# Moving a dozen output stores and three small transposes between queues in a block-sparse attention and gated MLP kernel

## The chip, the cores and the metric

The kernel runs on one core of one Trainium2 chip. The metric is the device time of one execution in microseconds (us); lower is better. The engines are TensorE (PE; its weight loads are listed as PEld), VectorE (DVE), ScalarE (ACT), GpSimd (POOL) and SyncE (SP). SP computes nothing: it issues DMAs.

## What is computed

Two stages in a row. The first is attention over 4 batches, 8 heads, 768 positions and 64 dimensions per head. Positions are grouped in 24 blocks of 32. A block of queries sees its neighbouring blocks, the first and the last block, and three sampled blocks; the first and the last query block see everything. The attention output, with its heads side by side, is the input x (4 x 768 x 512) of the second stage, a gated MLP:

```python
h = np.maximum(x @ w_in, 0.0)                       # 512 -> 1024
u, v = h[..., :512], h[..., 512:]
v_n = (v - mean(v)) / sqrt(var(v) + 1e-6)
v_s = einsum('ts,bsd->btd', w_spatial, v_n) + b_spatial[None, :, None]
out = (u * v_s) @ w_out                             # 512 -> 512, float32
```

## The kernel before

**Tiles.** Two heads make a pair; there are 16 pairs, four to a batch. The 768 positions are six chunks of 128. Keys and queries are loaded in float32, cast to bf16 and transposed, so that `kq` holds head dimension by position; 24 more rows of `kq` carry the block mask. The scores are computed transposed (keys on partitions), the exponential runs on ScalarE from PSUM into `a_all`, and a second product with `vv` (values with a column of ones beside them) gives the output and its row sum. DVE divides and writes `xn`, which has queries on partitions. For the MLP, x is needed transposed, as `xt` (features on partitions, 768 positions), one `xt` tile for each pair.

**Order.** The program is written out as slots, and each engine executes its own instructions in the order in which they are written. A slot holds one group of score matmuls, one group of value matmuls, and whatever tables attach to it: `at[s]` (before the MLP's steps of that slot), the MLP steps themselves (`run_queue(STEPS.get(s))`, one step is one matmul), and `late[s]` (behind them). Slots 0 to 35 are batch 0, slots 36 to 179 batches 1 to 3 with twelve slots to a pair, `S0` is 36.

**Batch 0** is cut in thirds of the query positions, 256 each. A *unit* is one pair and one third: units 0 and 1 are the two heads of pair 0 with its first two thirds; units 2 to 7 are pairs 1 to 3 with the first and the second third; units 8 to 11 are pairs 0 to 3 with the last third. `av_unit` ends with the division into `xn_ref[u]` (tag `xn3`, three buffers). `xtr_third(u)` then turns that x into its columns of `xt`: `xtr_pe` transposes chunk by chunk on TensorE into an unused part of the same PSUM tile, and DVE copies the result. The table `XT_AT` says behind which slot; a unit without an entry has slot `3 * u + 7`, which is 31, 34 and 37 for units 8, 9 and 10. The pairs of batches 1 to 3 take a different way: `xtr_dma` transposes all six chunks with one DMA on SP's queue.

**The MLP of batch 0** runs inside the slots of batches 0 and 1. The products `v4` and `v5` (chunks 4 and 5, the last third) are dealt at slot 42. One product is four matmuls, one for each pair, into one PSUM bank: slot 42 has the first of `v4` (pair 0), slot 43 the other three (pairs 1, 2, 3). Then come `u4` and `u5`, the spatial product (`s_product`), whose gated result is transposed by DMA on SP, and the output product (`o_product`). Each output product ends in a copy to an `osb` tile (six buffers) and a store of 256 KB to `out`. With `ST_ACT` empty for batches 0 and 1, their stores are on SP's queue. The six stores of batch 0 are written at slots 84, 88, 91, 93, 95 and 97, those of batch 1 at 136, 138, 140, 142, 143 and 145.

**SP's queue** carries nearly all DMAs. From slot 20 to 44 it has, in this order: the transpose of pair 4's k and q (`tr_dma`, L448, slot 20), the loads of pair 5 (slot 22), two transposes of the spatial weight (`ws_tr`, L593, slots 23 and 27), `tr_dma` of pair 5 (slot 31), the loads of pair 6 (slot 31), the third `ws_tr` (slot 31), the loads of pair 7 (slot 38), `tr_dma` of pair 6 (slot 40) and the loads of the output weight (slot 44).

**GpSimd's queue** has casts: k, q and v of each later pair (`cast`, L138), the spatial weight (`ws_cast`, L589), weights of the MLP, and the small reciprocal root of the normalisation (L661, L663). For pair p from 7 on, with g = 36 + 12 (p - 4), the casts are at slot g - 24 and the kq transpose at g - 20 (g - 16 for pairs 10 and 14). No DMA is issued from GpSimd.

The functions that the change touches, with what calls them:

Of the kernel before, what the change touches and what calls it, by code (L numbers as in the profile page):

```python
# [26 lines left out]
def kernel(  # L27
# [16 lines left out]
    nc = tc.nc  # L44
# [19 lines left out]
    TC = NCH // NT  # L64
    TW = TC * 128
# [154 lines left out]
    def dve_copy(o, i):  # L220
        nc.vector.tensor_copy(out=o, in_=i)  # L221
# [82 lines left out]
    def bank(nm="ps", tag=None):  # L304
        return psum.tile([128, 1024], BF16, tag=tag or moe_tag(), bufs=2 if tag else 1, name=nm)

    def tr(ps, c, in_):
        nc.tensor.transpose(out=ps[:, c * 128:(c + 1) * 128], in_=in_, identity=ident)  # L308

    def pair_of(src, c):  # L310
        return src[:, c].rearrange("p h d -> p (h d)")
# [143 lines left out]
    a_ref, av_ref, x_ref, xn_ref, xt_ref = {}, {}, {}, {}, {}  # L455
# [96 lines left out]
    def xt_tile(p):  # L552
        if p not in xt_ref:
            xt_ref[p] = work.tile([128, S], BF16, tag="xt", bufs=7, name="xt")
        return xt_ref[p]

    def xtr_pe(p, xn, c0, n, ps=None):
        if ps is None:
            ps = bank()
        for c in range(n):  # L560
            tr(ps, c, pair_of(xn, c))
        dve_copy(xt_tile(p)[:, c0 * 128:(c0 + n) * 128], ps[:, 0:n * 128])

    def xtr_third(u):
        t, p = UNITS[u]
        if t == "h":
            if p == 1:
                xtr_pe(0, xn_ref.pop(0), 0, 2 * TC)
        else:
            xtr_pe(p, xn_ref.pop(u), t * TC, TC, x_ref.pop(u))  # L570

# [42 lines left out]
    def product(n, lhs, rhs, last, done, w=512):  # L614
        ref = {}
        out = []
        for i in range(n):
            def run(i=i):
                if i == 0:
                    ref["ps"] = moe_ps(last)  # L620
                nc.tensor.matmul(out=ref["ps"][:, 0:w], lhsT=lhs(i), rhs=rhs(i),  # L621
                                 start=(i == 0), stop=(i == n - 1))
                if i == n - 1:
                    done(ref["ps"][:, 0:w])
            out.append(run)
        return out
# [3 lines left out]
    ST_ACT = [(), (), (4,), (0, 1, 2)]  # L630
# [3 lines left out]
    class Moe:  # L634
# [75 lines left out]
        def o_product(self, tcc):  # L710
            steps = []
            osb = {}
            parts = 2 if self.last and tcc == NCH - 1 else 1
            w = DM // parts
            for i in range(parts):
                cs = slice(i * w, (i + 1) * w)

                def done(ps, i=i, cs=cs):
                    if i == 0:
                        osb["t"] = work.tile([128, DM], FP32, tag="osb", bufs=6, name="osb")  # L720
                    on_act = (tcc + i) % 2 == 0 if self.last else tcc in O_ACT[self.b]
                    (act_copy if on_act else dve_copy)(osb["t"][:, cs], ps)
                    (nc.scalar if i or tcc in ST_ACT[self.b] else nc.sync).dma_start(
                        out=out[self.b].rearrange("(p c) d -> c p d", c=NCH)[tcc][:, cs],
                        in_=osb["t"][:, cs])
                steps += product(NDH, lambda d: self.gt[:, tcc, d, :],
                                 lambda d, cs=cs: w_out_t[:, d, cs], self.last, done, w)
            return steps
# [42 lines left out]
    def when(slot, *fns):  # L771
        at.setdefault(slot, []).extend(fns)

    def c(f, *a, **kw):
        return lambda: f(*a, **kw)
# [14 lines left out]
    when(2, staged)  # L790
    for p, sl in ((3, 18), (0, 21)):
        when(sl, c(tr_rest, p, 2 if p == 0 else 1))
    XT_AT = {1: 12, 3: 15, 5: 23, 11: 41}
    for u in range(1, len(UNITS)):
        late.setdefault(XT_AT.get(u, 3 * u + 7), []).append(c(xtr_third, u))
    late[12].append(c(tr_rest, 1))
# [134 lines left out]
```

## Time and profile before

| | |
|---|---|
| Median of 3 runs | 208.25 us (208.04 to 208.35) |
| The profiled execution's own time | 208.44 us |
| Its span in the profile | 206.7 us, 5245 instructions |
| Busy in the span | PE 97%, ACT 81%, DVE 64%, POOL 36% |
| DMA | 42.41 MB, nearly all on SP's queue |

The profile is one execution, recorded by the hardware. A row of a timeline has the start in us from the start of the span, the duration, the engine, the line of the program, the operation, the tile written and the tile read, and at the end, in brackets, how long the engine was idle before and what released it. Rows that follow each other with the same form are merged (x2). "SPq" is SP's queue of DMA issues: its duration is how long SP was held by the issue, not how long the data took. The view of one tile also gives the time from issue to landing as minimum, median and maximum. In the table of groups the figures behind the bar are total busy time, mean duration in ns, and idle time of the engine just before instructions of the group. Matmuls overlap, so the end of one lies beyond the start of the next.

### The profile page before, as it was taken

The page shows a single profiled execution, that of the slowest core. Times are in us where ns is not written, and L with a number is a line of the kernel's source. Part 1 is how long each engine was busy: PE and PEld are TensorE (multiplying, and loading weights), DVE is VectorE, ACT ScalarE, POOL GpSimd, SP SyncE. Part 2 cuts the span into 40 slices and gives each one's busy share as a digit, 9 for nine tenths or more (in the row PEclk, how much of TensorE's full clock was granted, in tenths as well). Part 3 has the DMA queues.
Part 4 walks back from the last instruction along what each step waited for, and adds up shares of the span by engine and source line. Part 5 has one row for each costly group of instructions (what it writes and reads, how often), then busy time and mean ns, then how long its engine had stood idle before and what let it go on. Part 6 is the DMA issues. An engine that isn't in the chain of part 4 may idle for free.

```text
span 206.7 us, 5245 instructions
## 1 busy us (share of the span) xinstructions
PE 201.2 (97%) x2122; PEld 126.4 (61%) x2122; DVE 131.4 (64%) x287; ACT 166.8 (81%) x222; POOL 74.4 (36%) x116
## 2 busy tenths in 40 slices
PE   8899999999999999999999999999999999999993
PEld 6679878766666666655655556655565656444441
DVE  7588797989654363648797355448686444576542
ACT  6999999999999999889999887998989883166021
POOL 6799799574680413210716401300202000013000
PEclk9999999999999999999999999999999999999999
DMA  5999999999999989999986749985101062960266
GB/s 140 355 362 359 326 410 270 235 250 333 267 357 201 251 242 203 325 308 271 285 113 172 174 89 264 205 236 127 38 3 38 0 92 51 162 235 0 44 163 251
DMA packets 66363, 42.41 MB, mean 205 GB/s; under 512 B 47524, under 2 KB 61220, under 8 KB 66340
## 3 DMA queue, kind: packets, MB, share of 16 engines
q1 hardware_dynamic: 65332, 40.71, 78.2%
q10 hardware_dynamic: 1008, 1.38, 1.8%
q8 instruction: 16, 0.26, 0.5%
q14 instruction: 7, 0.06, 0.1%
HBM read 24.38 MB, written 6.29 MB: 148 GB/s over the span
## 4 chain that ended last, share of the span: by engine, by line
PE 92%; DMA 3%; DVE 2%; SPq 1%; issue 0%; ACT 0%; ACTq 0%
PE ps_moe L621 33%; PE ps L491 23%; PE ps_av L542 13%; PE ps_t L621 8%; PE ps L478 6%; PE ps_sc L621 5%; PE ps_av L524 4%; DMA st_v<-in_v_dram 3%; DVE kq L221 1%; SPq L110 1%; PE ps L308 1%; PE ps_av L308 1%; DVE vv L138 1%; SPq L143 0%; DVE xn L507 0%
## 5 line engine op out<-in xcount | busy, mean ns | idle before, releaser
L495 ACT ACTIVATE a_all<-ps 128x768 bf16<-128x768 f32 x144 | 112.6, 812 | 11.7 <-PE ps L491 5.2
L491 PE MATMUL ps<-kq 88*128 88x384 bf16 x288 | 70.4, 325 | 0.0
L542 PEld LDWEIGHTS <-a_all 128*128 128x128 bf16 x864 | 45.2, 97 | 20.0
L542 PE MATMUL ps_av<-vv,a_all 128*128 128x65 bf16 x864 | 49.8, 193 | 0.0
L491 PEld LDWEIGHTS <-kq 88*128 88x128 bf16 x288 | 27.9, 97 | 29.0
L621 PE MATMUL ps_moe<-w_in_t,xt 128*128 128x512 bf16 x144 | 43.2, 378 | 0.0
L483 ACT ACTIVATE a_all<-ps 128x1024 bf16<-128x1024 f32 x36 | 34.0, 1026 | 1.5 <-PE ps L478 1.3
L621 PE MATMUL ps_moe<-vn,w_spt 128*128 128x512 bf16 x108 | 33.5, 378 | 0.0
L661 POOL TENSOR_SCALAR std<-mv 128x3 f32<-128x3 f32 (+1 forms) x9 | 2.9, 317 | 69.4 <-DVE mv L658 54.8
L138 POOL CAST nat<-st_k 128x768 bf16<-128x768 f32 (+2 forms) x18 | 13.8, 769 | 31.5 <-DMA st_k<-in_k_dram 30.4
L694 DVE SCALAR_TENSOR_TENSOR un<-ps_moe,b_col,un 128x512 bf16<-128x512 f32 x18 | 13.5, 749 | 14.8 <-PE ps_moe L621 14.8
L478 PE MATMUL ps<-kq 88*128 88x256 bf16 (+3 forms) x140 | 21.6, 275 | 1.2 <-DVE kq L221 0.5
L506 DVE RECIPROCAL rc<-ps_av 128x6 f32<-128x6 f32 (+1 forms) x36 | 6.7, 185 | 24.7 <-PE ps_av L542 23.2
L621 PEld LDWEIGHTS <-xt 128*128 128x128 bf16 x192 | 15.5, 98 | 7.8 <-issue 0.2
L507 DVE TENSOR_TENSOR xn<-ps_av,rc 128x384 bf16<-128x384 f32 (+1 forms) x36 | 18.5, 513 | 1.2
L621 PE MATMUL ps_moe<-w_out_t,gt 128*128 128x512 bf16 x60 | 18.1, 378 | 0.0
L657 DVE BATCH_NORM_STATS2 stats<-vn 128x6 f32<-128x512 bf16 x24 | 16.4, 684 | 1.3 <-ACT vn L652 0.9
L138 POOL CAST nat<-st_q 128x768 bf16<-128x768 f32 (+2 forms) x21 | 14.9, 708 | 3.8 <-DMA st_q<-in_q_dram 3.3
L478 PEld LDWEIGHTS <-kq 88*128 88x128 bf16 (+1 forms) x140 | 12.6, 97 | 5.6 <-DVE kq L221 1.6
L221 DVE COPY kq<-tt 64x1536 bf16<-64x1536 bf16 x24 | 15.1, 630 | 0.4
L188 DVE TENSOR_SCALAR vn<-ps_moe 128x512 bf16<-128x512 f32 x18 | 12.4, 686 | 4.7 <-PE ps_moe L621 4.6
L621 PEld LDWEIGHTS <-w_spt 128*128 128x128 bf16 x144 | 11.7, 98 | 5.2
(86 smaller groups left out, 208.1 us busy)
## 6 DMA issues: line engine op xcount, KB each, us to landing
st_v<-in_v_dram SPq DMA_DIRECT2D x16, 384.0 KB, 5.9
st_k<-in_k_dram SPq DMA_DIRECT2D x15, 384.0 KB, 5.0
out_dram<-osb SPq DMA_DIRECT2D x19, 256.0 KB, 2.7
st_q<-in_q_dram SPq DMA_DIRECT2D x12, 384.0 KB, 4.7
w_f<-in_moe_w_in_dram SPq DMA_DIRECT2D x6, 256.0 KB, 6.7
ws_f<-in_moe_w_spatial_dram SPq DMA_DIRECT2D x4, 384.0 KB, 7.5
out_dram<-osb ACTq DMA_DIRECT2D x4, 256.0 KB, 2.3
st_q<-in_q_dram SPq DMA_DIRECT2D x6, 128.0 KB, 5.6
```

The lines of the kernel that those rows point to most:

```text
L138: eng.tensor_copy(out=dst, in_=src)
L188: nc.vector.tensor_scalar(out=out, in0=in0, scalar1=s1, scalar2=s2, op0=o0, **kw)
L221: nc.vector.tensor_copy(out=o, in_=i)
L478: nc.tensor.matmul(out=ps[:, at:at + n * TW], lhsT=kq[0:kr, h, ci * 128:(ci + 1) * 128], rhs=kq[0:kr, h, qcols(t0, n)], start=True, stop=True)
L483: nc.scalar.activation(out=out, in_=ps, func=AF.Exp, scale=0.125)
L491: nc.tensor.matmul(out=ps[:, hf * 512:hf * 512 + HALF], lhsT=kq[0:KR, j % H, ci * 128:(ci + 1) * 128], rhs=kq[0:KR, j % H, S + hf * HALF:S ...
L495: nc.scalar.activation(out=a_ref["h", j][:, ci, :].rearrange("p (b c) -> p b c", b=2), in_=ps.rearrange("p (b c) -> p b c", b=2)[:, :, 0:H ...
L507: nc.vector.tensor_tensor(out=out, in0=ps[:, :, 0:D], in1=rc[:, 0:n].to_broadcast([128, n, D]), op=ALU.mult)
L542: nc.tensor.matmul(out=av_ref[j][:, qc, 0:VA], lhsT=a_ref["h", j][:, ci, qc * 128:(qc + 1) * 128], rhs=vv[p % NVV][:, h, ci, 0:VA], start= ...
L621: nc.tensor.matmul(out=ref["ps"][:, 0:w], lhsT=lhs(i), rhs=rhs(i), start=(i == 0), stop=(i == n - 1))
L657: nc.vector.bn_stats(out=stats, in_=self.vn[:, tcc, :])
L694: nc.vector.scalar_tensor_tensor(out=self.un[:, tcc, :], in0=ps, scalar=b_col[:, tcc:tcc + 1], in1=self.un[:, tcc, :], op0=ALU.add, op1=AL ...
```

## The change

Two edits. The stores of batches 0 and 1 (twelve, 256 KB each) are issued from GpSimd's queue; those of batches 2 and 3 stay where they were. And for units 8, 9 and 10 (pairs 0 to 2, last third) the x transpose on TensorE with its copy on DVE is replaced by one DMA transpose of two chunks each, on SP's queue; with it, these three move from behind slots 31, 34 and 37 to behind slots 29, 32 and 35, each the slot in which its `xn` is written. Unit 11 stays on TensorE, at slot 41.

```diff
@@ xtr_third
         if t == "h":
             if p == 1:
                 xtr_pe(0, xn_ref.pop(0), 0, 2 * TC)
+        elif t == 2 and p < 3:
+            nc.sync.dma_start_transpose(
+                out=xt_tile(p)[:, t * TW:(t + 1) * TW].rearrange("p (c n) -> p c n", c=TC),
+                in_=xn_ref.pop(u).rearrange("p c h d -> p (c h d)"))
         else:
             xtr_pe(p, xn_ref.pop(u), t * TC, TC, x_ref.pop(u))
@@ o_product
-                    (nc.scalar if i or tcc in ST_ACT[self.b] else nc.sync).dma_start(
+                    (nc.gpsimd if self.b < 2 else
+                     nc.scalar if i or tcc in ST_ACT[self.b] else nc.sync).dma_start(
                         out=out[self.b].rearrange("(p c) d -> c p d", c=NCH)[tcc][:, cs],
                         in_=osb["t"][:, cs])
@@ tables
-    XT_AT = {1: 12, 3: 15, 5: 23, 11: 41}
+    XT_AT = {1: 12, 3: 15, 5: 23, 8: 29, 9: 32, 10: 35, 11: 41}
```

## The prediction

> **What bounds the kernel now.** I read the page first, then the timelines of TensorE and of SP's DMA queue around the third query thirds of batch 0, then the tiles that the change touches. The page:
>
> ```profile
> PE 201.2 (97%) x2122; PEld 126.4 (61%) x2122; DVE 131.4 (64%) x287; ACT 166.8 (81%) x222; POOL 74.4 (36%) x116
> PE 92%; DMA 3%; DVE 2%; SPq 1%; issue 0%; ACT 0%; ACTq 0%
> L491 PE MATMUL ps<-kq 88*128 88x384 bf16 x288 | 70.4, 325 | 0.0
> ```
>
> TensorE is 92% of the chain that ended last, and the largest group of its matmuls (the scores of batches 1 to 3) has 0.0 us of idle time ahead of it: nothing that TensorE needs comes late. Two things follow. Work taken from SP, DVE or GpSimd buys nothing unless TensorE has less to do. And a wait put into TensorE's stream costs its whole length, since no later idle time can give it back.
>
> SP's DMA queue executes in program order, and in the stretch that the change touches it is full:
>
> ```profile
> 33.57 5.47 SPq L593 DMA_TRANSPOSE w_spt<-ws_b  x2
> 39.13 2.89 SPq L448 DMA_TRANSPOSE tt<-nat  x1
> 42.07 0.58 SPq L110 DMA_DIRECT2D st_k<-in_k_dram  x1
> ...
> 43.20 0.47 SPq L110 DMA_DIRECT2D st_v<-in_v_dram  x1
> 44.13 2.84 SPq L593 DMA_TRANSPOSE w_spt<-ws_b  x1
> 47.01 0.58 SPq L110 DMA_DIRECT2D st_k<-in_k_dram  x1
> ...
> 48.74 3.45 SPq L448 DMA_TRANSPOSE tt<-nat  x1
> ```
>
> The order is that of the slots in the code: the first two transposes of the spatial weight (slots 23 and 27), the kq transpose of pair 5 (slot 31), the three loads of pair 6 (slot 31), the third weight transpose (slot 31), the loads of pair 7 (slot 38), the kq transpose of pair 6 (slot 40).
>
> **Part one: three x transposes go from TensorE to SP's queue.** Units 8, 9 and 10 are pairs 0, 1 and 2 of the last query third. Their x is read by the products v4 and v5, which are dealt at slot 42: one matmul in slot 42 (pair 0), three in slot 43 (pairs 1, 2 and 3). In TensorE's timeline these are the first two L621 rows here:
>
> ```profile
> 45.38 0.38 PE L621 MATMUL ps_moe<-w_in_t,xt 128*128 128x512 bf16 x1
> 45.60 0.49 PE L491 MATMUL ps<-kq 88*128 88x384 bf16 x2
> 45.93 0.35 PE L542 MATMUL ps_av<-vv,a_all 128*128 128x65 bf16 x6
> 46.11 0.81 PE L621 MATMUL ps_moe<-w_in_t,xt 128*128 128x512 bf16 x3
> 46.76 0.49 PE L491 MATMUL ps<-kq 88*128 88x384 bf16 x2
> ```
>
> Three matmuls take 46.76 - 46.11 = 0.65, or 0.22 each: pair 0 is needed at 45.38, pair 1 at 46.11, pair 2 at 46.33.
>
> Removed: two transposes on TensorE and one copy on DVE for each of the three units. One of each:
>
> ```profile
> 36.33 0.27 PE L308 MATMUL ps_av<-ident,xn 128*128 128x128 bf16 x2
> 38.18 0.27 DVE L221 COPY xt<-ps_av 128x256 bf16<-128x256 bf16 x1
> ```
>
> At most 3 x 0.27 = 0.8 us of TensorE (the 0.27 holds the drain of the pipeline too, which overlaps what follows) and 0.8 us of DVE. I credit neither separately: below, the end is set by when a transfer lands, not by how early TensorE gets there.
>
> Added: three DMA transposes of two 128x128 blocks on SP, after slots 29, 32 and 35. Their place among the other entries is what matters. Unit 8 comes before the kq transpose of pair 5. Units 9 and 10 come behind it, behind pair 6's loads and **behind the third weight transpose**, ahead of pair 7's loads. Their inputs are ready early, so they don't wait for data; what holds the weight transpose ahead of them is a cast on GpSimd:
>
> ```profile
> 34.74 0.42 DVE L507 TENSOR_TENSOR xn<-ps_av,rc 128x256 bf16<-128x256 f32 x1
> ...
> 40.57 0.43 DVE L507 TENSOR_TENSOR xn<-ps_av,rc 128x256 bf16<-128x256 f32 x1
> 41.02 3.08 POOL L589 CAST ws_b<-ws_f 128x768 bf16<-128x768 f32 x2 [2.00 <-DMA w_spt<-ws_b]
> ```
>
> Unit 8's xn is there at 35.16, unit 10's (the last of the three) at 41.00, the cast at 44.10. No row shows a two-block transpose. The nearest are the six-block x transposes of the later batches, and one eight-block transpose of the gated product in the tail with nothing else in flight:
>
> ```profile
> L573 SPq DMA_TRANSPOSE xt<-xn x12: 1210/1246/1831, 59.6 to 176.9; - x12
> DMA to landing us min/median/max: 2.7/3.7/5.8
> gt<-un SPq DMA_TRANSPOSE x1, 3.1
> w_spt<-ws_b SPq DMA_TRANSPOSE x1, 5.7
> ```
>
> SP is held 1.21 to 1.83 for six blocks. A third of the blocks may take a third of that, 0.40; I take 1.2, as the shortest and the median of the row are the same, which looks like a fixed price. From issue to landing I take 3.1, between the row's 2.7 and its median 3.7, because blocks are few but a weight transpose is just ahead. The sum along SP's queue, with gaps of 0.05 as in the rows:
>
> - The second weight transpose ends at 39.04. Unit 8: 39.1 to 40.3, landing 42.2, ahead of its need at 45.38. No stall there.
> - Kq transpose of pair 5: 40.35 + 2.89 = 43.24. Loads of pair 6 (43.67 - 42.07 = 1.60): 43.3 to 44.9.
> - Third weight transpose (cast long done): 44.95 + 2.84 = 47.8.
> - Unit 9: 47.85 to 49.05, landing 50.95, needed at 46.11.
> - Unit 10: **49.1** to 50.3, landing **52.2**, needed at 46.33.
>
> TensorE is in order. Behind the waiting product stand the scores of slot 44 and all else; ScalarE can finish what is in its two PSUM buffers and then has nothing. So the second matmul of slot 43 moves from 46.33 to 52.2, **5.9 us**, and by the page all behind it moves as well.
>
> Bounds: with SP held 0.40 each, unit 8 ends at 39.5, the kq transpose at 42.4, the loads at 44.1, the weight transpose at 47.0, and unit 10 is issued at 47.45; at 2.7 it lands at 50.15, a stall of 3.8. The weight transpose ahead (5.7 from 44.13) lands at 49.8, so little less is possible on shared queues. With 1.83 each, unit 10 is issued near 50.4; at 5.8 it lands at 56.2, a stall of 9.9. I stay at 5.9, nearer the low end: the 5.8 belongs to a transfer three times as large behind loads and a kq transpose.
>
> Further back on SP, pair 7's loads begin at 50.35 and the kq transpose of pair 6 at 50.35 + (48.74 - 47.01) = 52.1, 3.3 later than before. Its readers come behind the stalled matmul and are 5.9 later, so it costs nothing more. The kq transpose of pair 5, 1.2 later, is read for slot 48, also behind the stall. The three xn3 buffers are kept until their transfer has read them; unit 11 takes the one of unit 8, free since 42.2.
>
> **Part two: twelve output stores go from SP's queue to GpSimd's.** What SP sheds:
>
> ```profile
> L723 SPq DMA_DIRECT2D out_dram<-osb x20: 332/409/1528, 80.3 to 203.5; - x20
> SPq L723 <- DVE osb L221: 5.7, 4, 2.0
> ```
>
> That is 12 x 0.41 = 4.9 us of issue and up to 5.7 us of waits, all in stretches where TensorE waits for nothing. Gain: 0. On GpSimd each store waits for the copy to its osb, and what is queued behind waits with it. The nearest case is batch 0's fifth store (slot 95), ahead of pair 11's casts (slot 96):
>
> ```profile
> 85.65 0.83 POOL L138 CAST nat<-st_k 128x768 bf16<-128x768 f32 x1 [5.80 <-DMA st_k<-in_k_dram]
> 88.28 0.59 ACT L224 ACTIVATE osb<-ps_moe 128x512 f32<-128x512 f32 x1
> 93.91 2.84 SPq L448 DMA_TRANSPOSE tt<-nat  x1
> 108.24 1.13 DVE L221 COPY kq<-tt 64x1536 bf16<-64x1536 bf16 x2
> ```
>
> The store can go at 88.87. If GpSimd is held for one to two us (its price is in no row; SP's longest is 1.53), the two casts that the kq transpose reads run from 90.4 to 92.1, still ahead of that transpose at 93.91. Even 5 us later, its result would be there before the split at 108.24. In batch 1, pair 15's casts stand behind the fifth store in the same way, with 139.03 against 156.05:
>
> ```profile
> 139.03 1.48 SPq L448 DMA_TRANSPOSE tt<-nat  x1
> ...
> 156.05 1.13 DVE L221 COPY kq<-tt 64x1536 bf16<-64x1536 bf16 x2
> ```
>
> DVE may be held by GpSimd's work on a store. The trace shows the size of such a thing:
>
> ```profile
> L221 DVE COPY kq<-tt x24: 540/554/1214, 36.2 to 156.6; 64x1536 bf16<-64x1536 bf16 x24
> ```
>
> The same copy takes 0.55 or up to 1.21; I put the difference, 0.66, down to GpSimd at work beside it. Twelve would be 7.9 us of DVE, which is 64% busy; TensorE would see only what makes an eviction late. Bounds 0 and 7.9, taken 0, since the collisions that before has already leave TensorE's groups without idle time. The Trainium skill (SBUF — State Buffer, "SBUF: two separate sides") speaks against this part: descriptors of a GpSimd-issued DMA are written by GpSimd, and a DVE operation in a two-port mode locks it out, so that a 0.62 us DMA took about 3.1 us. By that figure, as an estimate, each store would be some 2.5 us late; nothing on the path waits for a store, so the sum would stay. No row of before shows a store from that queue.
>
> **Sum.** The profiled execution took 208.44, span 206.7, so 1.74 lie outside. 206.7 + 5.9 + 1.74 = 214.3; the median of the runs, 208.25, is 0.19 less, so **214.2**.
>
> **Rivals.**
>
> *The clock falls in the stall.* TensorE would be idle from about 46.1 to 50.95, run one matmul, and idle again to 52.2. The kernel's start shows what a start from rest costs:
>
> ```profile
> 0.97 2.63 PE L182 MATMUL wps<-warm 128*128 128x128 bf16 x23 [0.97 <-DVE past L162]
> ...
> 4.97 0.63 PE L478 MATMUL ps<-kq 128*128 128x256 bf16 x4
> ...
> 14.35 0.61 PE L308 MATMUL ps<-ident,nat 128*128 128x128 bf16 x8
> 14.80 0.60 PE L478 MATMUL ps<-kq 88*128 88x256 bf16 x4
> ```
>
> One drain of 0.22 left out, the 23 matmuls follow each other at 0.110 us, the eight of the same size at 14.35 at 0.056: half the rate. At 4.97 four matmuls take what they take at 14.80, so full rate is back after 4.0 us. Half rate for 4.0 us costs 2.0 us: 216.2. Against it: no pause in this trace is long enough to show a fall. The pause of 4.8 us is longer than the 4.0 us of the rise, but a fall may be slower; I give it two fifths of the cases with a stall. The Trainium skill (TensorE: Matmul & The Clock Gate, "What's actually happening") has the gate fall to half after an idle window of about 3.4 us that runs freely, and rise after a busy one. By that rule an idle stretch of 4.8 us holds a whole window in some two of five positions.
>
> *The x transposes arrive in time, and it is faster.* It decides at 46.33: if unit 10 is landed by then, no stall arises. For this SP must have issued units 9 and 10 by 43.6, that is ahead of the third weight transpose. Then TensorE has up to 0.8 less to do, the drain not counted some 0.3: 207.9. Against it: the trace keeps slot order on SP throughout, and by it the weight transpose can't start before 44.10.
>
> *Stores on GpSimd cost as well.* If half of the 7.9 us of collisions reached evictions that TensorE waits for, in stretches where it has no slack, some 2 us would come on top: 216.2.
>
> *The stall is hidden in part.* If SP gives small transposes away much faster and they overtake the weight transpose on the DMA engines, unit 10 lands near 48.5: 2.2 us, 210.5.
>
> **How the numbers follow.** Stall without a fall of the clock 0.47; with it 0.30; stall and costly stores 0.08; partly hidden 0.06; in time and faster 0.06; the two edits cancel within what can be told 0.03. A measurement of this kernel can tell about 0.2% from no change. Faster 0.06, same 0.03, slower 0.91. The range leaves out the last two cases, the lower one partly, and the far end of the stall's bound: 211.6 to 217.8, from a stall of 3.3 to the clock case with a stall of 7.5.
>
> **What would show it.** TensorE idle by 4 to 7 us before the L621 product at slot 43, released by the DMA xt<-xn; before it, in SP's timeline, unit 9 and 10's transposes directly behind the third weight transpose; ScalarE idle at the same time; all stretches behind shifted by the same amount, with TensorE's share of the span near 94%. GpSimd shows twelve stores in two groups and no wait of TensorE near them. If the first matmul on pair 1's x has no wait, the forecast is wrong at its root; if matmuls behind the stall follow at half rate for some us, the clock rival holds; if x lands much under 2.7 us, the size is wrong.

## The result and the profile after

| | before | after |
|---|---|---|
| Median (6 runs each) | 208.36 us | 216.33 us |
| Ratio, 95% interval | | 1.0368 (1.0347 to 1.039) |
| Profiled execution, its span | 208.44, 206.7 | 216.39, 214.6 |

The change makes the kernel 3.7% slower. Of the runs below, e1, e6, e10 and e11 each had one or two executions more than 1.5% above the fastest of the same kernel; these are in the medians, but not in the ratios. The page of after:

```profile
PE 201.2 (94%) x2083; PEld 126.8 (59%) x2116; DVE 130.4 (61%) x284; ACT 166.7 (78%) x222; POOL 80.7 (38%) x128
PEclk9999999995799999999999999999999999999999
PE 73%; DMA 17%; POOL 4%; SPq 2%; issue 1%; ACT 0%; DVE 0%; ACTq 0%; DVEq 0%
L625 PE MATMUL ps_moe<-w_in_t,xt 128*128 128x512 bf16 x129 | 40.9, 389 | 6.2 <-DMA xt<-xn 5.7
```

TensorE's share fell from 97% to 94%, and one group, the products on `xt`, now has 6.2 us of idle time ahead of it, nearly all of it waiting for the DMA that writes `xt`. The row of the granted clock has a dip in the tenth slice. The chain that ended last was 92% TensorE; it is now 73%, because it leaves TensorE at this wait and goes back along SP's queue to the cast and the load of the spatial weight. SP's timeline there:

```profile
34.18 6.63 SPq L597 DMA_TRANSPOSE w_spt<-ws_b  x2
40.90 1.20 SPq L570 DMA_TRANSPOSE xt<-xn  x1
42.19 1.46 SPq L448 DMA_TRANSPOSE tt<-nat  x1
43.70 0.88 SPq L110 DMA_DIRECT2D st_k<-in_k_dram  x1
...
45.71 2.96 SPq L597 DMA_TRANSPOSE w_spt<-ws_b  x1
48.77 2.48 SPq L570 DMA_TRANSPOSE xt<-xn  x2
```

The transposes of units 9 and 10 (the last row) stand behind the third weight transpose, as the code has them. By the view of the DMAs from 48 to 56 us that weight transpose landed 5.7 us after its issue, at 51.4, and unit 9's x 3.1 us after its own, at 51.9. TensorE's timeline, with one row from a narrower window (the second x row, which the merged row of three hides) and one weight load:

```profile
45.79 0.35 PE L542 MATMUL ps_av<-vv,a_all 128*128 128x65 bf16 x6
51.88 1.59 PE L625 MATMUL ps_moe<-w_in_t,xt 128*128 128x512 bf16 x3 [5.74 <-DMA xt<-xn]
...
52.44 1.03 PE L625 MATMUL ps_moe<-w_in_t,xt 128*128 128x512 bf16 x2
53.27 0.85 PE L491 MATMUL ps<-kq 88*128 88x384 bf16 x2
```

```profile
52.43 0.13 PEld L625 LDWEIGHTS <-xt 128*128 128x128 bf16 x2 [0.46 <-DMA xt<-xn]
```

Pair 1's matmul starts at 51.88 instead of 46.11. Pair 2's starts at 52.44 instead of 46.33, which is 6.1 us later, after its own short wait. Two score matmuls then take 0.85 us where before they took 0.49: the clock is down. The next view has one row for each stretch, with the length, the busy time of the five engines in the order PE, PEld, DVE, ACT, POOL, the granted clock, the DMA share and GB/s. The stretches are cut where the clock changes in this trace:

```profile
45.71:49.12 3.41, 0.43 (x8) 0.24 (x6) 1.20 (x3) 1.57 (x3) 0.98 (x3) 1.00 0.93 308
49.12:52.53 3.41, 0.65 (x2) 0.20 (x3) 0.00 (x0) 0.00 (x0) 1.62 (x2) 0.50 0.81 180
52.53:55.95 3.42, 3.42 (x15) 1.54 (x16) 2.12 (x4) 0.81 (x1) 0.00 (x0) 0.50 0.98 286
```

The clock fell while TensorE waited and stayed at half until 55.95. From 52.44 on that is 3.51 us at half rate, a loss of half of it, 1.76.

Behind this nearly everything is shifted by one constant. I use one row of ScalarE's timeline as a **marker**: a group of four exponentials in batch 2 that has the same form in every kernel here. Before, then after:

```profile
124.44 3.58 ACT L495 ACTIVATE a_all<-ps 128x768 bf16<-128x768 f32 x4 [0.41 <-PE ps L491]
```

```profile
132.26 3.58 ACT L495 ACTIVATE a_all<-ps 128x768 bf16<-128x768 f32 x4 [0.41 <-PE ps L491]
```

The marker is 7.82 later, of the 7.95 between the two profiled executions. 6.11 of it is the later start of pair 2's matmul, and 1.71 is left for the clock, against the 1.76 just worked out. The stores on GpSimd (group and timeline):

```profile
L728 POOL DMA_DIRECT2D out_dram<-osb x12 | 6.8, 570 | 26.3 <-ACT osb L224 16.9
```

```profile
96.98 0.54 POOL L728 DMA_DIRECT2D out_dram<-osb  x1 [1.33 <-ACT osb L224]
97.51 0.83 POOL L138 CAST nat<-st_k 128x768 bf16<-128x768 f32 x1
```

GpSimd waits for each copy and is then held for about 0.54 us; pair 11's casts follow at once.

### The profile page after: what moved, and what is told of

Same layout as the page of the kernel before. It is cut to its first block, busy times and chain, and to the rows that moved or that the text cites. A ratio compares the mean times of both kernels' runs of the same rounds, so it can differ in the third digit from the quotient of the medians.

```text
span 214.6 us, 5203 instructions
## 1 busy us (share of the span) xinstructions
PE 201.2 (94%) x2083; PEld 126.8 (59%) x2116; DVE 130.4 (61%) x284; ACT 166.7 (78%) x222; POOL 80.7 (38%) x128
## 4 chain that ended last, share of the span: by engine, by line
PE 73%; DMA 17%; POOL 4%; SPq 2%; issue 1%; ACT 0%; DVE 0%; ACTq 0%; DVEq 0%
PE ps_moe L625 27%; PE ps L491 22%; PE ps_av L542 12%; PE ps_t L625 7%; PE ps_sc L625 5%; DMA ws_f<-in_moe_w_spatial_dram 4%; POOL ws_b L593 4%; DMA w_spt<-ws_b 3%; DMA st_v<-in_v_dram 3%; DMA w_f<-in_moe_w_in_dram 3%; DMA st_k<-in_k_dram 3%; DMA xt<-xn 1%; SPq L597 1%; SPq L110 1%; POOL rstd L667 1%
## 5 line engine op out<-in xcount | busy, mean ns | idle before, releaser
L625 PE MATMUL ps_moe<-w_in_t,xt 128*128 128x512 bf16 x129 | 40.9, 389 | 6.2 <-DMA xt<-xn 5.7
L625 PE MATMUL ps_moe<-vn,w_spt 128*128 128x512 bf16 x97 | 30.1, 378 | 0.3
L138 POOL CAST nat<-st_k 128x768 bf16<-128x768 f32 (+2 forms) x18 | 14.6, 813 | 18.5 <-DMA st_k<-in_k_dram 18.5
L625 PE MATMUL ps_moe<-w_out_t,gt 128*128 128x512 bf16 x55 | 16.9, 378 | 0.1
L728 POOL DMA_DIRECT2D out_dram<-osb x12 | 6.8, 570 | 26.3 <-ACT osb L224 16.9
```

The costliest lines, as they stand in the source:

```text
L138: eng.tensor_copy(out=dst, in_=src)
```

## The experiments

Short diffs are against the kernel before unless said otherwise. "The x edit" is the hunk in `xtr_third` with the new `XT_AT`, and "the stores edit" is the hunk in `o_product`.

### e1_stores_only

```diff
-                    (nc.scalar if i or tcc in ST_ACT[self.b] else nc.sync).dma_start(
+                    (nc.gpsimd if self.b < 2 else
+                     nc.scalar if i or tcc in ST_ACT[self.b] else nc.sync).dma_start(
```

> Only the twelve stores of batches 0 and 1 go from SP's queue to GpSimd's; x as before. Theory A (all of the loss is the late x of pairs 1 and 2 and the clock behind it): 208.3 us, within 0.3 of before, no wait of TensorE between 80 and 160 us. Rival B (stores on GpSimd hold DVE or the casts, and TensorE with them): 209.3 to 210.3.

Median 208.77, ratio 1.0023 (0.9999 to 1.0047). The marker stands at 124.33, 0.11 earlier than before. So the stores edit does not explain the 8 us. A price up to 1 us is not excluded by the times, and TensorE has no wait between 80 and 160 us in the trace. One execution of the twelve took 214.87 us; no trace of it was kept, so its cause stays open.

### e2_x_only

The x edit alone.

> Only the three x transposes go to SP's queue, at the new slots; the stores stay on SP's queue. Theory A: 216.3 us, the same as with both edits, with a wait of 5.7 us before the first matmul on pair 1's x and half rate behind it. Rival B: 1 to 2 us less than with both edits, 214.3 to 215.3.

Median 216.94, ratio 1.0403 (1.0375 to 1.0431): the whole loss comes with the x edit, and the 1 to 2 us less that rival B asked for are not there. TensorE:

```profile
50.94 0.61 PE L625 MATMUL ps_moe<-w_in_t,xt 128*128 128x512 bf16 x1 [4.82 <-DMA xt<-xn]
52.15 1.03 PE L625 MATMUL ps_moe<-w_in_t,xt 128*128 128x512 bf16 x2 [0.59 <-DMA xt<-xn]
```

Here the two waits stand apart: pair 1, then pair 2.

### e4_unit8_only

```diff
+        elif u == 8:
+            nc.sync.dma_start_transpose(...)   # as in the x edit
-    XT_AT = {1: 12, 3: 15, 5: 23, 11: 41}
+    XT_AT = {1: 12, 3: 15, 5: 23, 8: 29, 11: 41}
```

> Of the three, only pair 0's last third is transposed by DMA (behind slot 29, ahead of the kq transpose of pair 5 on SP's queue); pairs 1 and 2 stay on TensorE at slots 34 and 37; stores as before. Theory A (a transposed x costs nothing where it lands ahead of its need): it lands near 44 us, needed at 45.3: 208.2 us, within 0.3 of before. Rival D (a DMA transpose of x costs by itself, by delaying all that is behind it on SP): 209 or more.

Median 208.67, ratio 1.0026 (1.0008 to 1.0045). No wait for x, as expected: unit 8 is the one ahead of the third weight transpose. The profiled execution has its marker at 124.02, 0.42 early; one new wait stands ahead of it, where a chunk transpose comes to TensorE before DVE has divided:

```profile
38.90 0.28 PE L308 MATMUL ps_av<-ident,xn 128*128 128x128 bf16 x2 [0.39 <-DVE xn L507]
```

The profiled execution took 208.33 us and does not show where the median's 0.3% comes from. It does show that in this execution one transpose of this kind, in a place where its data is in time, cost next to nothing.

### e3_filler, e7_filler34, e9_filler30

Both edits, and useless matmuls on TensorE ahead of the waiting product, so that the stall stays but TensorE is busy in it: 24, 34 and 30 of them.

```diff
+    NFILL = 24          # 34, 30
+    def keep_busy():
+        ps = psum.tile([128, 512], FP32, tag=moe_tag(), bufs=1, name="wps")
+        for _ in range(NFILL):
+            nc.tensor.matmul(out=ps, lhsT=warm, rhs=oh[:, 0:512], start=True, stop=True)
+        moe_tags.rotate(1)
+    when(43, keep_busy)
```

> Both edits, and 24 matmuls of 512 columns on a table of zeros, written into TensorE's stream in slot 43 ahead of the waiting product, to a PSUM bank that nobody reads: 24 x 0.216 = 5.2 us of useless work in the wait of 5.7. Theory A (the half rate behind the wait is the clock, which fell because TensorE idled): the clock stays, the matmuls behind take 0.22 each at once, and the time falls by 2.0 to 214.3 us although work was added. Rival C (the half rate has another cause: operands, PSUM or DVE late after the wait): no change, 216.3 us, or more.

Median 217.25, ratio 1.0414 (1.0387 to 1.0441): the gain of 2 us did not come. The fill was too short, since x landed a microsecond later than in after, and a pause of 1.80 was left (TensorE's timeline, then its windows):

```profile
45.77 5.34 PE L786 MATMUL wps<-oh,warm 128*128 128x512 bf16 x24
52.91 1.13 PE L626 MATMUL ps_moe<-w_in_t,xt 128*128 128x512 bf16 x3 [1.80 <-DMA xt<-xn]
```

```profile
50.71:54.12 3.41, 1.47 (x7) 0.48 (x6) 0.04 (x1) 0.00 (x0) 0.00 (x0) 1.00 0.59 119
54.12:57.54 3.42, 3.20 (x21) 1.78 (x21) 2.08 (x4) 1.58 (x2) 0.00 (x0) 0.50 1.02 334
```

The clock fell all the same. TensorE had been busy for 1.47 of the 3.41 us before the fall. Of the other three executions only the time and the mean clock are on record. Two have a mean of 0.997 and 1.000, which leaves no room for such a fall (3.41 us at half clock are 0.008 of the span), and still took 216.52 and 217.19 us. So a clock that stays up did not by itself bring the time down; where these two lost it is not known.

> Both edits, with 34 in place of 24 useless matmuls ahead of the waiting product: 34 x 0.216 = 7.3 us, from 45.8 to 53.1, past the landing of the x of pair 2 (52 to 52.9 so far), so that TensorE never pauses. The product begins 53.1 - 46.1 = 7.0 later than before, 1.2 later than with both edits alone. Theory A (the clock falls because TensorE pauses; with 24 a pause of 1.8 was left): clock 1.00 throughout, 215.4 us, 1 us less than with both edits although TensorE works on nothing for 7 us. Rival C (the half rate behind the wait does not come from the pause): 217.4 us.

Median 217.62, ratio 1.0445 (1.0415 to 1.0475).

> Both edits with 30 useless matmuls ahead of the waiting product: 6.5 us, from 45.8 to 52.3, about to the landing of the x of pair 2. With 34 the scores of batches 1 to 3 ran 7.24 later than before at full clock, against 7.82 with both edits alone, but the last transposes of the tail landed late and took that back. Theory A (the pause lowers the clock): scores 6.4 to 7.0 later than before, full clock from the start to the tail; 215 us if the tail is as before, up to 217 if it is late again. Rival C: scores 7.8 or more later, half rate behind the wait.

Median 216.83, ratio 1.0432 (1.0399 to 1.0464). In these two no pause is left, and the clock stays up. TensorE in e9, then one window, then its marker, and last the product in e7:

```profile
45.61 6.64 PE L786 MATMUL wps<-oh,warm 128*128 128x512 bf16 x30
52.08 0.81 PE L626 MATMUL ps_moe<-w_in_t,xt 128*128 128x512 bf16 x3
```

```profile
54.00:56.00 2.00, 2.00 (x28) 1.32 (x26) 1.76 (x4) 1.65 (x4) 0.00 (x0) 1.00 0.97 272
```

```profile
130.42 3.58 ACT L496 ACTIVATE a_all<-ps 128x768 bf16<-128x768 f32 x4 [0.41 <-PE ps L492]
```

```profile
53.35 0.81 PE L626 MATMUL ps_moe<-w_in_t,xt 128*128 128x512 bf16 x3
```

Pair 1's matmul is 0.20 later than in after, yet the marker is 1.84 *earlier*: its shift against before is 5.98, to 0.01 us the delay of the product (52.08 - 46.11 = 5.97). In e7 the product starts at 53.35 and the marker is 131.68, and both are 7.24 late. So up to the marker theory A holds to 0.01 us, and rival C, with half rate behind the wait, is excluded. The total missed: both medians lie above those of the changed kernel, because both profiled executions lose time in the tail: the spans grew by 8.9 (e7) and 7.4 (e9), 1.7 and 1.4 more than their markers. TensorE in the tail of e7 and of e9:

```profile
211.34 0.61 PE L626 MATMUL ps_sc<-w_out_t,gt 128*128 128x256 bf16 x4 [1.77 <-DMA gt<-un]
```

```profile
209.81 0.61 PE L626 MATMUL ps_sc<-w_out_t,gt 128*128 128x256 bf16 x4 [1.49 <-DMA gt<-un]
```

The last transposes of the gated product land later there, TensorE waits for them, and most of what the clock saved is used up. In both traces one fetch of instructions lies in that stretch, and in before, after and e3 none does; that the two belong together was not tested.

### e12_after_again

The changed kernel, unaltered, once more.

> Both edits, unchanged, on the chip of the other runs of this group: 216.3 us, scores of batches 1 to 3 7.8 later than before, half rate for some 4 us behind the wait.

Median 215.97, ratio 1.0373 (1.0322 to 1.0424). The profiled execution (214.78, span 213.0) is a shorter one. The first two weight transposes held SP for 5.48 instead of 6.63, so x came earlier: pair 2's matmul starts at 51.04. And only one stretch of the clock is at half:

```profile
47.33:50.74 3.41, 0.22 (x1) 0.10 (x1) 0.00 (x0) 0.00 (x0) 1.63 (x2) 1.00 0.93 198
50.74:54.16 3.42, 3.33 (x15) 1.41 (x15) 1.96 (x4) 0.81 (x1) 0.00 (x0) 0.50 0.81 268
```

The marker is 6.23 late. All ten executions of this kernel, in both sets, had a mean granted clock below 0.993 (0.976 to 0.992), and their spans, 212.9 to 215.9, are in the main longest where it is lowest. Before has 0.997 to 1.000 in both sets. A fall in the tail alone, as in the profiled executions of e7 and e9, left 0.994 and 0.995.

### e5_ws2_late

The x edit, and the third weight transpose moved behind units 9 and 10 on SP's queue.

```diff
-    for i, sl in enumerate((23, 27, 31)):
+    for i, sl in enumerate((23, 27, 36)):
         when(sl, c(ws_tr, i))
```

> The three x transposes on SP's queue, stores as before, and the third transpose of the spatial weight moves from slot 31 to slot 36, so that it stands behind units 9 and 10 instead of ahead of them. Theory A (place in SP's queue sets the wait): units 9 and 10 are issued at 45.7 and 46.9, land 3.1 later, at 48.8 and 50.0; the second matmul of slot 43 begins 3.7 to 4.0 late: 212.2 us if the clock holds, 214.2 if it falls. Rival E (the transfers are slow by themselves, wherever they stand): 216 us.

Median 215.31, ratio 1.0341 (1.031 to 1.0371). SP, TensorE and the windows:

```profile
44.52 2.50 SPq L570 DMA_TRANSPOSE xt<-xn  x2
```

```profile
48.95 1.46 PE L625 MATMUL ps_moe<-w_in_t,xt 128*128 128x512 bf16 x3 [2.95 <-DMA xt<-xn]
```

```profile
44.61:48.02 3.41, 1.39 (x15) 0.81 (x12) 1.49 (x4) 2.53 (x4) 1.90 (x3) 1.00 1.01 341
48.02:51.43 3.41, 2.48 (x12) 1.17 (x13) 0.95 (x2) 0.34 (x1) 1.24 (x2) 0.50 1.08 194
51.43:54.84 3.41, 3.41 (x21) 1.74 (x20) 1.18 (x3) 1.81 (x3) 0.00 (x0) 0.50 1.41 322
```

The wait shrinks from 5.74 to 2.95, which shows that the weight transpose ahead made about half of it. It does not vanish, because pair 6's loads are still ahead, and pair 1's x, issued right behind them at 44.52, took 4.4 us to land, where the forecast had 3.1. The time, 215.31, lies between the forecasts of theory A with a fall (214.2) and of rival E (216): place sets one half of the wait, and slow landings have a part in the rest. The median gains only 1.6 us on e2's (in the ratio, 0.6%), because even this shorter pause brought the clock down, for 6.8 us: pair 2's matmul is 3.05 late and the marker 5.69.

### e6_reorder

The x edit; SP's order changed so that x is in time: the second and third weight transposes at slots 41 and 53, pair 6's loads at slot 36 instead of 31.

> The three x transposes on SP's queue, stores as before, and SP's order changed so that they come early: the second transpose of the spatial weight moves from slot 27 to 41, the third from 31 to 53, the loads of pair 6 from 31 to 36. Theory A: unit 10 is issued near 41.3, when its data are ready, and lands at 44.4, ahead of 46.3: no wait, no fall of the clock; 208.1 us, 0.3 less than before for six transposes fewer on TensorE, and at most the same. Rival D (DMA transposes of x cost by themselves, by delaying what follows on SP): 209 or more, with TensorE or DVE waiting on a kq transpose or a weight transpose.

Median 212.56, ratio 1.0171 (1.0131 to 1.0211). The stall is gone (the product on xt starts at 45.48 with no wait), but later, on DVE and then on TensorE:

```profile
77.62 0.55 DVE L221 COPY kq<-tt 64x1536 bf16<-64x1536 bf16 x1 [2.82 <-DMA tt<-nat]
86.94 0.55 DVE L221 COPY kq<-tt 64x1536 bf16<-64x1536 bf16 x1 [4.18 <-DMA tt<-nat]
```

```profile
88.84 0.65 PE L625 MATMUL ps_moe<-w_out_t,gt 128*128 128x512 bf16 x2 [2.02 <-DVE osb L221]
```

The new order left SP idle from 46.86 to 49.23 and pushed its later entries back: the kq transpose of 74.19 before is issued at 79.25. DVE waits for it, output copies queue behind DVE, TensorE waits 2.02 for one, and the clock falls for 3.4 us. The marker is 3.86 late. This is what rival D asked for.

### e8_defer

Both edits, and the fourteen MLP steps of slots 43 to 50 dealt to slots 51 to 64, so that TensorE has scores to do until x lands.

```diff
-    STEPS = {... 43: 3, 44: 3, 45: 0, 46: 2, 47: 1, 48: 2, 49: 1, 50: 2, 51: 0, 52: 2, ...}
+    STEPS = {... 43: 0, 44: 0, 45: 0, 46: 0, 47: 0, 48: 0, 49: 0, 50: 0, 51: 1, 52: 3, ...}
```

> Both edits; SP's order untouched, but the 14 matmuls of the products that batch 0 has in slots 43 to 50 move to slots 51 to 64, one more in each. TensorE reaches the first matmul on pair 1's x near 52, when it has landed. Until then the slots hold scores and values alone, and ScalarE's exponentials (0.81 each) set their pace: eight slots in 6.5 in place of 7.1 us, and 14 x 0.217 = 3.0 us paid later. Theory A (only the order on TensorE makes the wait): 208.4 - 0.6 + 3.0 = 210.8 us, no wait on x. Rival E (late x costs the same wherever it is used): 215 or more.

Median 217.64, ratio 1.0434 (1.0401 to 1.0467).

```profile
53.66 0.85 PE L491 MATMUL ps<-kq 88*128 88x384 bf16 x2 [1.75 <-DMA xt<-xn]
65.50 0.38 PE L625 MATMUL ps_moe<-vn,w_spt 128*128 128x512 bf16 x1 [1.62 <-DVE vn L188]
```

The work that was to fill the stall ran out before x had landed, and the steps packed together behind it came to the spatial product ahead of the normalisation. Two pauses of less than 1.8 us, and after each of them 3.4 us at half clock. The marker is 8.88 late. The forecast of 210.8 missed, and rival E's time is met, though by another way than it said.

### e10_order2 and e11_order2_pool

A second order: the x edit; pair 6's loads at slot 28, pair 5's kq transpose at 36 (its two copies to `kq` at 46 and 49), the weight transposes at 23, 39 and 53, pair 9's first copy two slots later. e11 adds the stores edit.

> The three x transposes on SP's queue, stores as before, and a second order for SP. The first order had x in time (scores 0.14 earlier than before up to slot 100) but left SP idle for 2.4 us and made a later kq transpose land late, which cost 4. Now: loads of pair 6 at slot 28, kq transpose of pair 5 at slot 36 with its splits at 46 and 49, weight transposes at 39 and 53, the first split of pair 9 two slots later. Theory A (nothing is lost where every landing on SP stays ahead of its reader): 208.1 us, within 0.4 of before. Rival D (three more transposes, 3.6 us, are more than SP's queue can take before pair 9's kq transpose): 209 to 212, with DVE waiting for a kq transpose between 75 and 90 us.

Median 211.02, ratio 1.0112 (1.0092 to 1.0132).

> The second order for SP together with both edits, the stores on GpSimd's queue included. Theory A: as without the stores, 208.1 us, within 0.4. Rival F (SP's relief from the stores pays where SP is late): 0.3 or more below the same order with the stores on SP.

Median 212.26, ratio 1.0131 (1.0084 to 1.0178): no difference from e10 can be told, so rival F is not shown. The 208.1 of theory A was missed in both. The product at slot 43 waits for nothing in either. In e11, DVE, TensorE and the view of line 570:

```profile
44.89 0.42 DVE L507 TENSOR_TENSOR xn<-ps_av,rc 128x256 bf16<-128x256 f32 x1 [2.25 <-DMA xt<-xn]
```

```profile
45.37 0.28 PE L308 MATMUL ps_av<-ident,xn 128*128 128x128 bf16 x2 [0.83 <-DVE xn L507]
```

```profile
L570 SPq DMA_TRANSPOSE xt<-xn x3: 1196/1197/1852, 37.9 to 41.1; - x3
DMA to landing us min/median/max: 4.3/5.3/6.9
```

Unit 11's division needs one of three `xn3` buffers, and these are held until the DMA transposes have read them. Issued right behind three loads, the transposes took 4.3 to 6.9 us, DVE waited 2.25, and TensorE waited for DVE; the marker is 1.45 late. In e10's profiled execution (213.39 us) the same wait is longer (3.87 on DVE), and its marker is 4.15 late. TensorE there, and the windows around the pause:

```profile
47.42 0.28 PE L308 MATMUL ps_av<-ident,xn 128*128 128x128 bf16 x2 [2.45 <-DVE xn L507]
```

```profile
43.34:46.75 3.41, 1.63 (x9) 0.63 (x7) 0.00 (x0) 2.53 (x4) 3.24 (x4) 1.00 1.25 280
46.75:50.17 3.42, 2.75 (x26) 1.62 (x27) 3.11 (x6) 1.77 (x3) 2.56 (x4) 1.00 1.08 231
```

This pause of 2.45 us lies across two windows, and the clock did not fall. A fourth buffer was not tried, and no order tried beats the kernel before.

## Why the prediction was right, and where it was not

The time was within the range and on the forecast side, at the figure of the second case (stall and falling clock, 216.2); the other case with that figure, costly stores, is excluded by e1 and e2. The likeliest case, 214.2, which the sum gives, was not what happened.

**The place and the cause: right.** The wait is at slot 43, released by the DMA that writes `xt`, with units 9 and 10 behind the third weight transpose. e2 shows that the x edit alone does it, e4 that unit 8 alone does not, e5 that the wait shrinks by half when the order of the two is turned round.

**The size of the stall: right, partly by luck, since errors cancel.** Pair 2's matmul moved by 6.1, forecast 5.9. SP reached unit 8 at 40.90 (39.1 in the sum), since the two weight transposes held it for 6.63 (5.47 before). It then needed 1.46, not 2.89, for the kq transpose. Unit 10 was issued at 50.06 (49.1), and its weights were loaded at 52.43, 2.4 us after the issue instead of 3.1. The price of 1.2 on SP for each small transpose was right for after, 1.19 to 1.20, but it is the low end and not fixed: single ones held SP for 1.83 in e12 and for 2.38 in e3.

**The clock: the failed step is its chance.** Two fifths of the cases with a stall was too low. Half rate followed the stall in both profiled executions of the changed kernel, and the mean clocks of the other eight fit it. The parts add up for each kernel in which pair 2's matmul is late (us against before; the clock's loss is half of the time at half rate behind that matmul):

| kernel | pair 2's matmul later by | clock's loss | sum | marker later by |
|---|---|---|---|---|
| after | 6.11 | 1.76 | 7.87 | 7.82 |
| after, again | 4.71 | 1.56 | 6.27 | 6.23 |
| e2 | 5.82 | 1.97 | 7.79 | 7.74 |
| e5 | 3.05 | 2.73 | 5.78 | 5.69 |
| e3 (TensorE busy in part of the stall) | 7.11 | 1.71 | 8.82 | 8.77 |
| e9 (TensorE busy in all of it) | 5.97 | 0 | 5.97 | 5.98 |
| e7 (the same) | 7.24 | 0 | 7.24 | 7.24 |

The price of 2.0 was near, though the start of the kernel that it was taken from varies: in before four matmuls at 4.97 ran at full rate, in e1 four of the same form at 5.03 still took 1.01 us, and the clock came up at 6.88. The chance rested on a fall that may be slower than the rise. The windows above say otherwise: the clock changed on a grid of 3.41 us, and it fell after windows in which TensorE was still busy for 0.43, 0.22, 1.47 and 1.39 us (after, e12, e3, e5). A pause of 4.8 us covers at least 2.4 of one such window wherever it lies, so at most 1.0 is left busy, less than in e3 and e5. By these traces the fall was not a matter of luck, and the forecast should have been the 216.2. The Trainium skill (TensorE: Matmul & The Clock Gate, "What's actually happening") has the clock fall after an idle window of about 3.4 us, by which two fifths come out too; the grid agrees, the condition does not.

**Stores at no cost: right within what can be told** (e1: 0 to 1 us). GpSimd was held 0.54 for a store, below the 1 to 2 us allowed. The median landing of the twelve was 4.4 us (4.0 in e1), against 2.8 for the same twelve on SP's queue in before. The delay of 2.5 us per store worked out from the Trainium skill (SBUF — State Buffer, "SBUF: two separate sides") did not show in full: the landings are 1.2 to 1.6 us later, and the longest of the twelve held GpSimd for 0.79. Whether the locked port makes the landings late, no run here shows. Nothing on the path waited for a store, as the prediction had it.

**Missed: the buffers.** "Unit 11 takes the one of unit 8, free since 42.2" was wrong as to the time: SP issued unit 8 only at 40.90, and its transfer landed 3.1 us later, at 44.0. In after, DVE waited for it:

```profile
44.08 0.43 DVE L507 TENSOR_TENSOR xn<-ps_av,rc 128x256 bf16<-128x256 f32 x1 [1.01 <-DMA xt<-xn]
```

That lies ahead of the longer stall and cost nothing there; in e11, without the stall, it became the first wait.

## What to carry to other kernels

Before a transfer goes onto a DMA queue that executes in order, list what stands ahead of it at that very place, with the data that each of those entries waits for; then look at who else holds its buffers until it has landed. Price a stall of TensorE as its length plus half of the stretch at half clock that follows (the table above), and reckon with that stretch even after pauses of 1.6 to 2.0 us (e3, e6, e8), though the 2.45 us of e10 had none. Then look at the whole time: in e7 and e9 most of what the clock saved was lost again in the tail. When the queue is reordered to cure one late transfer, look for the next late one: e6, e10 and e11 each cured the first wait and met another.

## What the chip showed that was not expected

The clock does not need a wholly idle window. With the traces cut along the grid, eight falls ahead of the tail came after windows of 3.41 us with 0.2 to 1.8 us of work in them, and the falls in the tails of eight traces after 0.2 to 1.3. Every window at full clock with up to 1.47 us of work was followed by a fall. Of seven windows with 1.5 to 1.9, only one was, with 1.77 (e8); after's tail with 1.52 and e10 with 1.63 had none. So the border lies near 1.5, and the busy time alone does not settle it there. Nor does the clock rise after just any work: in e5 it stayed at half after 2.48 of 3.41, and so it did at the start of e1. The least busy windows with a rise behind them are at the start of e5 and e9, with 2.67 and 2.76.

At its shortest, a DMA transpose of two 128x128 blocks holds SP for 1.2 us (1.19 in after), as long as one of six blocks (1.21 in before): by these times three small ones cost three times as much of the queue as one large one.

The same program issued the same entries on SP's queue up to 2.2 us apart in two executions (unit 8 at 40.90 and at 38.67, unit 9 at 48.77 and at 47.38). The changed kernel waits for the last of these entries, and its times in the second set spread over 1.4% where before's lie within 0.4%. How much of the spread comes from the queue and how much from the clock was not separated.
